# Transposing the softmax output P by DMA in three of four head groups, in a two-layer attention and FFN kernel on one Trainium2 core

## The chip, the cores and the metric

The kernel runs on one core of one Trainium2 chip. The metric is the time of one execution on the device, in microseconds (us). Before the change the median of three runs is 2704.88 us (2704.35 to 2705.86). A change of less than about 0.2%, 5.4 us, can't be told from none.

The core has five engines that run side by side and meet through semaphores: PE (TensorE) multiplies matrices and writes to PSUM, DVE (VectorE) and ACT (ScalarE) work on PSUM and SBUF, POOL (GpSimd) works on SBUF, and SP (SyncE) issues DMAs here. Each engine takes its instructions in order.

## What is computed

Two passes of the same two layers over 2048 rows of 576 numbers: attention with a recurrent memory, then a gated FFN. The attention works on 64 segments of 32 rows. Each segment sees 8 memory rows and itself, 40 rows in all, and the first 8 rows of its output are the memory of the next segment, so segments of one layer run one after another.

```python
for s in range(n_seg):                                  # 64 segments
    h = concat([mem, x[:, s*32:(s+1)*32]], axis=1)      # 8 + 32 rows
    q, k, v = (einsum('btd,dhe->bhte', h, W) for W in (Wq, Wk, Wv))   # 32 heads of 128
    scores = where(mask, einsum('bhqe,bhke->bhqk', q, k) * scale, -1e9)
    p = softmax(scores)
    o = einsum('bhqk,bhke->bhqe', p, v)
    o = einsum('bhte,hed->btd', o, Wo)
    mem = o[:, :8]
    outs.append(o[:, 8:])
...
x = x + A(layernorm(x)); x = x + B(layernorm(x))        # B: (silu(x w1) * (x w3)) w2, F = 4608
x = x + A(layernorm(x)); x = x + B(layernorm(x))
```

## The kernel before, in words

**Steps.** The kernel walks 72 steps `t`. Step `t` does segment `t` of the first attention and segment `t - 8` (`LAG`) of the second, so that their two recurrences run at the same time. In steps 8 to 63 both are there (56 steps "with two layers", `both(t)`); the first and last 8 steps have one. In a two-layer step the 40 rows of one layer's segment lie in partitions 0 to 39 and those of the other in 64 to 103, and the columns of a matmul are 80 instead of 40. `role(t)` alternates and says which places in the key rows the two layers use. The FFN of 128 rows at a time is woven between the steps.

**A group.** The 32 heads of a step are four groups `g` of eight (`NG`, `GH`). For each group, `step(t)` makes these nodes: QK and QKt (projections, two units a group), SC (scores into a PSUM bank), then on DVE the add of the mask (`sm_add`), the maximum and its subtraction (`sm_max`), on ACT the exponential (`sm_exp`), on DVE the sum, its reciprocal (`sm_sum`) and the scaled write of P as bf16 into the tile `PB` (`sm_pb`). `PB` has 128 key columns for each head; only those columns that belong to a row's own layer are written, the others must be zero, and so POOL clears the buffer after each use (`pb_zero`). There are two `PB` buffers.

**Transposing P.** The product of P and V needs P with keys in partitions. `ptr` (TR) does this on PE: eight matmuls a group with the P of one head as the stationary side and the tile `fold` (two identity matrices, one above the other) as the moving side, 40 columns each. The sum of both layers' rows comes out in one PSUM bank; since a key belongs to one layer only, `pt_ev` (PTe) copies the bank twice into the tile `PTS`, each time scaled by a 0 or 1 for each partition (`slots`) so that each layer keeps its own keys. ACT or DVE makes these copies, whichever the planner chooses. `pv` (PV) multiplies V and `PTS`, then come the copy into `OT` and the output projection WO, WOt.

**The order.** `make_nodes` lists all nodes with their needs, buffers and a planned duration. PE's order isn't planned: it is written out as a string of letters, `FIRST + FOUR * 11 + LAST`, one letter for a node (Q, q, S, T, P, O, o for attention, F, f, W, w for the FFN, X, x, V, v, G, g for V, and so on). `FOUR` holds four steps. `plan` takes that order and places the nodes of the other engines by their planned durations; the order within ACT, DVE, POOL and SP is the result, and the tile framework adds the semaphores. "AD" nodes may go to ACT or DVE.

**Queues around the change.** SP issues the weight loads of the FFN (`load_w13`: four DMAs, `load_w2`: one) into two buffers each, when PE has freed them, and the loads of rows of x. The planner has one queue "DMA" for it. POOL's queue issues the residual rows and the stores and holds the memsets of `PB`.

**PE's tile shapes.** A matmul with 128 rows and 128 columns of weights uses the whole array. Tails with 64 rows go in pairs side by side (64*128), and some others are split into two halves of 64 columns (128*64) where the neighbours already use that shape. Node modes such as `full/col` let `plan` pick the shape that the neighbours have.

Of the kernel before, what the change touches and what calls it, by code (L numbers as in the profile page):

```python
# [34 lines left out]
POOLS = {"bank": 8, "qkt": 4, "sme": 2, "pb": 2, "pts": 1, "ot": 4,  # L35
# [158 lines left out]
def ewh(*ns):  # L194
# [5 lines left out]
    "maQQQqqQqqSQqTqSqQQQqSSvVXxPTPTOPOTOoPooOoQqqqqQQSQqqvSVQQTQSqqPQOTSPoXTOPToxPOOooQqqqqQQSQQSvqVQTqqQSQqPSaOTPTO"  # L200
    "PTooPOOooQQqqqqQSQVvSqqQQQqqQTSSPXTOPTOPoToxPOOooQQpQqqVvqqSnQQSfFFqqfQQqSTQqfPFTWPSFTOOooPFTffPOOooWQqqqqQQFSQF"
    "SQffqVvqqQWTQSFxfqfQFSPXTWPFTfOPOTFPOOooooWQqfqQQSFQfqqVvSQqqfFWTQqfQSFPQqfTOSPFOTWPFTOPfoooOoFfqqQQQSWQqqvVSFfq"
    "qQQTWqqSQQPTSOoPbaOTXPxTOPooxOoXqqpQQQSVqqnQvfFSTQqqQQPSFfqqfQTFOPSWTFfPOOTFPWOooooffFQQQqqqWSGFfgqQQqfFSTQPQQqq"
    "qfFSWGTSfgGPFggTGOPOTFPOOooooWVvfqqQQQSFqqffFQQWTSFfqqQPQfqqSFQWTOfPSTaFoOPWOTFPffFOoooWQQqqqqQSbQgqqGSQQTQPQTgq"
    "qSGSOPGggTGPOTOPoooOoQqqppQQQSvqqVnnQQqqSFSffqTFQPQqWTFSPffOwTFPOTFPOWOwooooFffqqQQQSWwQFfgqqGSFqqfQQTWQPQSFffqq"
    "FGTgSwPGfggTGPFTOPOWOOowoooFqqfQQwWQaQfqqSFSvVfqqQFQTFqqfPQTQwSWFSfPOOTFPwTWffFPOOooooWwqqqQQQbSQqqgqGSQTQPQQqgq"
    "TSGSGPggGTOPOTOPoooOo"
# [5 lines left out]
LAST = (  # L213
    "QQpQqqqQSqQpnQqqVvTSSnQFffqqFPQTOwPoSWTffFPFTOPOOoooFqqqfQQwWQQfqfSFSFqGQQqqgTQQPWwFqgfTSSGGPFfggfFTGOPOTWPOOwoF"
    "oooFfqqfQQQwvSqqVQQWQqqSFTSqfqQPQWTOPSwFTFPffOTOwPWOooooFFqqffQQwQQqqvSWVSFqqfQQTWPQTqqSVQvPOSTbOPxwOoTooPOoXqQp"
    "QpqqvVQSQqqnQnSQQqqFTSfqfPQTOPSFTFPOWTOPwOooooFqffqQQQSQQqqqvVSTQQqqFSffqFPQWSwTFPffTOPFOTwPOOoWoooFqfqqQQQFSQfq"
    "xvXVwWSTFPQffqqQWQTSwFFPfqqQOSwWTFOPffTFPOWOwooooFQQvfqqVqqQSQWFSwFffqqQQQSTWQqPqTPSOTOPowOToboPxOoXqqqQQQpSvVqq"
    "qQQSnQTFfqQFSPfqQOSTFfPowTFPfOTOPFOfooowQQqqqfQQSqFSVvqqQwQFTSQffqqQPFTSXPwTOPOTFPOOooooFfxfVvqqQQQSQqqqfQSFQqqq"
    "QSTQwSPFTOffPFTOPwTOPfooOooFQqqqQQSqqqQQSQvVQTSfFQqqPwTFSPfTOFPOTOPoofOoopwFnfffFFwFwfffFFFwffFFwffFFwffFFwfFffF"
    "wFwfffFFFfww"  # L220
# [11 lines left out]
def make_nodes(em, nseg, pools, o=Opt, dma_bw=230e3, load_bw=400e3):  # L232
# [26 lines left out]
    ld_m0 = node("ACT", 0.1, em.load_m0(), prio=-90, name="m0", lat=2.5)  # L259
    ld_t = [load("ldt", kb(3 * R64, 4096), -10.0, em.load_tails(0)), node("ACT", 0.1, em.load_tails(1), prio=-120, name="ldt", lat=6.0)]  # L260
    node("ACT", 0.1, em.load_tails(2), prio=-80, name="ldt", lat=6.0)
# [48 lines left out]
    def v_nodes(name, t, k, prio, tail_at, emit, strips, deps, tail_deps, free):  # L310

        modes = ("col", "quad") if strips[0][3] == R64 else ("c32", "oct")
        b = banks()
        m_ = node("PE", 8 * 0.2158, emit(b, False), deps=deps, prio=prio, mode=modes[0], acq=b, name=name)
        n = node("PE", 0.2158, emit(b, True), deps=deps + tail_deps, prio=prio + tail_at, mode=modes[1], acq=b, name=name + "t")
        reads_ht.setdefault(t, []).extend([m_, n])
        for r in (0, 1):
            outs = em.v_parts(strips, r)
            b[r].users = len(outs)
            for p0, width, row, blk in outs:  # L320
                e = node("AD", (0.49, 0.6), em.v_ev(b[r], p0, width, row, blk), deps=[m_, n] + free.get(blk // 2, []), prio=prio + 0.01 * (blk // 2),
                         rel=[b[r]], name=name + "e")
                vx_ev.setdefault((name, t, blk // 2), []).append(e)
        return [m_, n]
# [16 lines left out]
    def vg_out(t, g, b, deps, row):  # L341

        return [node("AD", (0.49, 0.6), em.v_ev(b[r], row, R64, row, 2 * g + r), deps=deps, prio=t + o.vm + 0.01 * g + (0.05 if row == 0 else 0.0), rel=[b[r]],
                     name="VGe") for r in (0, 1)]

    def vx_pair(t, prio):
# [5 lines left out]
        for k in ((0, 1) if both(t) else (0,)):  # L352
            v_nodes("VX", t, k, prio + 0.01 * k, o.vxt, (lambda k: lambda b, tail: em.vx(t, k, b, tail))(k), em.vx_strips(t, k), deps, [], free)

    def step(t):
# [17 lines left out]
        for g in range(NG):  # L373
# [25 lines left out]
            pbs = node("DVE", w, em.sm_pb(t, g, sme, pb), deps=[d], prio=pf, acq=[pb], rel=[sme], name="pb", lat=0.125 if nl == 2 else 0.225)  # L399
# [26 lines left out]
            me[f"SC{g}"], me[f"TR{g}"], me[f"PV{g}"], me[f"WO{g}"] = sc, tr, pv, wo  # L426
# [100 lines left out]
    def x_in(g):  # L527
        xn = Slot("xn")
        ld = node("DMA" if g else "ACT", 0.8 if g else 0.1, em.load_xn(g, xn), deps=reads_ht.get(4 * g - 3, [])[:1], prio=4 * g - 3.0 if g else -100, acq=[xn],
                  name="ldxn", lat=2.5)  # L530
# [31 lines left out]
SW = 2 * QW  # L562

# [4 lines left out]
class Emitter:  # L568
# [431 lines left out]
    def sm_pb(self, t, g, sme, pb):  # L1000
        def f(n):
            for kd, key, c0, w in self.p_at(t):
                rs = slice(64 * kd, 64 * kd + QW)
                X, rec = self.T.SME[rs, sme.i], self.T.STAT[rs, sme.i]
                self.v("tensor_tensor", self.T.PB[rs, pb.i, :, c0:c0 + w], X[:, :, key:key + w],
                       rec.unsqueeze(2).to_broadcast([QW, GH, w]), op=ALU.mult)
        return f

    def pb_zero(self, pb):
        return lambda n: self.ch("POOL", self.nc.gpsimd.memset(self.T.PB[:, pb.i], 0.0))  # L1010
# [4 lines left out]
    def ptr(self, t, g, pb, b):  # L1015

        def f(n):
            for j in range(GH):
                self.mm(self.bk(b)[:, j * QW:(j + 1) * QW], self.T.PB[0:104, pb.i, j, :], self.T.fold[0:104, :], True, True)
        return f  # L1020

    def pt_ev(self, t, g, m, b, pts):

        def f(n):
            src = self.bk(b)[:, 0:GH * QW]
            if not self.both(t):
                w = 4 * QW
                self.cp(n, self.T.PTS[:, pts.i, 0, m * w:(m + 1) * w], src[:, m * w:(m + 1) * w])
                return
            dst = self.T.PTS[:, pts.i, m, :]  # L1030
            keep = self.T.slots[:, role(t), m ^ role(t):(m ^ role(t)) + 1]
            if n.by == "ACT":
                self.act(dst, src, ACT.Copy, scale=keep)
            else:
                self.v("tensor_scalar", dst, src, keep, None, op0=ALU.mult)
        return f

    def pv(self, t, g, pts, b):
        def f(n):
            nq = self.nq(t)  # L1040
            for j in range(GH):
                self.mm(self.bk(b[j // 4])[:, (j % 4) * nq:(j % 4 + 1) * nq], self.T.V[:, self.head(g, j) // 4, (self.head(g, j) % 4) * E:(self.head(g, j) % 4 + 1) * E],
                        self.T.PTS[:, pts.i, 0:nq // QW, j * QW:(j + 1) * QW], True, True)
        return f

# [66 lines left out]
    def yts(self, t, ls, tail):  # L1112
        def f(n):
            yT, _ = self.yT(t)
            for li in ls:
                j = (t - LAG * li) % 4
                c0 = self.ycol(t, self.kind(t, li), False)
                if not tail:
                    self.cp(n, self.T.YTS[:, li, 0:4, j * SEG:(j + 1) * SEG], yT[:, 0:4, c0:c0 + SEG])
                else:  # L1120
                    self.v("tensor_tensor", self.T.YTS[R64:P, li, 4, j * SEG:(j + 1) * SEG], yT[0:R64, 4, c0:c0 + SEG],
# [3 lines left out]
    def post_tr(self, li, g, b):  # L1125
        def f(n):

            for db in (4, 3, 2, 1, 0):
                d0 = min(db * P, D - P)
                self.mm(self.bk_bf(b, D)[:, d0:d0 + P], self.T.YTS[:, li, db, :], self.T.ident[:, 0:P], True, True, is_transpose=True)  # L1130
# [79 lines left out]
def kernel(  # L1210
# [41 lines left out]
    T.fold = sp.tile([P, QW], BF, name="fold")  # L1252

    T.slots = sp.tile([P, 2, 2], F32, name="slots")

# [29 lines left out]
    nc.gpsimd.memset(T.fold[:], 0.0)  # L1285
    for r in (0, R64):
        nc.gpsimd.affine_select(out=T.fold[:], in_=T.fold[:], compare_op=ALU.not_equal, fill=1.0, base=-r,
                                pattern=[[-1, QW]], channel_multiplier=1)

    nc.gpsimd.memset(T.slots[:], 0.0)  # L1290
    for e, kd, lo, hi in ((0, 1, 24, 80), (1, 0, 72, 112)):
        inside, outside = T.slots[:, e, kd:kd + 1], T.slots[:, e, 1 - kd:2 - kd]
        nc.gpsimd.memset(inside, 1.0)
        nc.gpsimd.affine_select(out=inside, in_=inside, compare_op=ALU.is_ge, fill=0.0, base=-lo, pattern=[[0, 1]], channel_multiplier=1)
        nc.gpsimd.affine_select(out=inside, in_=inside, compare_op=ALU.is_ge, fill=0.0, base=hi - 1, pattern=[[0, 1]], channel_multiplier=-1)
        nc.gpsimd.tensor_scalar(outside, inside, -1.0, 1.0, op0=ALU.mult, op1=ALU.add)

# [54 lines left out]
```

## Time and profile before

| what | value | how to read it |
|---|---|---|
| median of three runs | 2704.88 us | unprofiled comparisons |
| profiled execution | 2708.0 us, span 2705.0 us | the span is from first to last instruction |
| granted PE clock | 0.997 of full | no throttling |
| PE, DVE, ACT, POOL busy | 2618.6, 2097.7, 1401.6, 334.1 us | PE is the busiest by far |
| transposes on PE, 104*128 and 104*64 | 1816 and 976 records | fold,PB in the rows; split ones count twice |
| copies PTS on ACT | 315 at 531 ns, 97 at 303 ns | two-layer and one-layer steps |
| copies PTS on DVE | 133 at 550 ns, 31 at 320 ns | the same |
| memset of PB on POOL | 288 at 951 ns | one for each group |
| DMA queue of SP | 305.43 MB, 38.5% of 16 engines | nearly all weight loads |
| a repeated period of four steps | 157.03 us | 1170.72 to 1327.75 us in the trace |

Busy times on PE are unions of pipelined matmuls, so the length of one record (180 ns and more) is a latency. What a matmul costs in a stream is the distance between the starts of two neighbours.

### The profile page before, as it was taken

The numbers are of one execution on the slowest core, as the hardware profiler recorded it, in microseconds if no ns is written. First come the engines' busy times: TensorE is split into PE (matmuls) and PEld (weight loads), VectorE is DVE, ScalarE is ACT, GpSimd is POOL, SyncE is SP. The second block draws the span as 40 slices with busy tenths as digits, with TensorE's granted clock in tenths as the row PEclk, the third lists the DMA queues.
The fourth block names the chain that finished last, engine by engine and source line by source line (L and its number), as shares of the span: only waits on it lengthen the run. The fifth ranks groups of instructions, "written<-read, shape, count | busy, mean of one in ns | idle before, by whom it ended". The sixth has DMA issues, their size and how long they took to land.

```text
span 2705.0 us, 135792 instructions
## 1 busy us (share of the span) xinstructions
PE 2618.6 (97%) x60482; PEld 2272.3 (84%) x60523; DVE 2097.7 (78%) x5423; ACT 1401.6 (52%) x3978; POOL 334.1 (12%) x411
## 2 busy tenths in 40 slices
PE   5999999999999999999999999999999999999998
PEld 4788888888888888888888888888888888888886
DVE  5777887787788778777877877787777777777876
ACT  2655554554555555554555555455545546554452
POOL 1111110110111011011101101010111101011110
PEclk9999999999999999999999999999999999999999
DMA  9064524244342434434243433423343342334457
GB/s 316 7 182 118 158 82 128 80 119 116 104 124 85 116 90 119 117 108 128 76 119 88 127 108 108 134 80 110 94 124 106 108 139 70 112 93 130 129 166 245
DMA packets 478171, 321.99 MB, mean 119 GB/s; under 512 B 26024, under 2 KB 467760, under 8 KB 476944
## 3 DMA queue, kind: packets, MB, share of 16 engines
q1 hardware_dynamic: 474048, 305.43, 38.5%
q8 instruction: 473, 7.75, 1.2%
q0 software_dynamic: 3024, 6.93, 0.9%
q10 hardware_dynamic: 512, 0.94, 0.2%
q14 instruction: 114, 0.93, 0.1%
HBM read 308.49 MB, written 2.36 MB: 115 GB/s over the span
## 4 chain that ended last, share of the span: by engine, by line
PE 80%; DVE 9%; ACT 6%; issue 2%; DMA 2%; SPq 1%; POOL 0%; ACTq 0%; DVEq 0%; POOLq 0%
PE bank L591 80%; ACT V L594 3%; DVE STAT L597 2%; DVE PTS L597 2%; ACT PTS L594 1%; DVE V L597 1%; DVE SME L597 1%; DVE PB L597 1%; DMA W<-in_A_Wk_dram 1%; DVE HTT L597 1%; SPq L600 1%; DMA W<-in_B_w_dram 1%; ACT HT L594 0%; ACT QKT L594 0%; DMA WV<-in_A_Wv_dram 0%
## 5 line engine op out<-in xcount | busy, mean ns | idle before, releaser
L591 PEld LDWEIGHTS <-W 128*128 128x128 bf16 (+2 forms) x31904 | 1258.2, 100 | 128.8 <-issue 68.7
L591 PE MATMUL bank<-HT,W 128*128 128x80 bf16 (+3 forms) x23040 | 799.9, 196 | 16.8 <-issue 7.3
L591 PE MATMUL bank<-XTB,W 128*64 128x256 bf16 (+5 forms) x8864 | 662.6, 263 | 5.9 <-DMA W<-in_B_w_dram 3.0
L594 ACT ACTIVATE QKT<-bank 128x256 bf16<-128x256 f32 (+2 forms) x1524 | 349.5, 311 | 363.5 <-PE bank L591 320.7
L1010 POOL MEMSET PB<- 128x1024 bf16 x288 | 273.9, 951 | 1944.5 <-PE bank L591 1242.7
L591 PE MATMUL bank<-OT,WO 128*128 128x80 bf16 (+2 forms) x11520 | 401.6, 198 | 2.2 <-issue 1.8
L594 ACT ACTIVATE V<-bank 32x512 bf16<-32x512 f32 (+1 forms) x609 | 347.8, 586 | 90.4 <-PE bank L591 81.6
L591 PEld LDWEIGHTS <-WO 128*128 128x128 bf16 (+1 forms) x11520 | 376.8, 102 | 13.7 <-issue 4.4
L591 PE MATMUL bank<-WV,HT 128*32 128x512 bf16 (+5 forms) x3728 | 362.3, 381 | 3.8 <-issue 2.2
L591 PE MATMUL bank<-W2C,HTT 128*128 128x288 bf16 (+1 forms) x2776 | 318.4, 286 | 2.9 <-issue 1.8
L597 DVE TENSOR_REDUCE STAT<-SME 104x8 f32<-104x320 f32 (+1 forms) x576 | 274.0, 476 | 25.2 <-ACT SME L594 18.9
L597 DVE TENSOR_TENSOR PB<-SME,STAT 40x128 bf16<-40x128 f32 (+4 forms) x912 | 275.5, 336 | 9.7
L594 ACT ACTIVATE HTT<-bank 128x512 bf16<-128x512 f32 (+1 forms) x324 | 175.3, 550 | 185.9 <-PE bank L591 183.9
L591 PEld LDWEIGHTS <-HT 128*32 128x32 bf16 (+4 forms) x3768 | 164.1, 99 | 119.5 <-issue 20.3
L597 DVE SCALAR_TENSOR_TENSOR XR<-bank,XR 128x288 f32<-128x288 f32 x576 | 243.7, 448 | 23.3 <-PE bank L591 17.4
L591 PEld LDWEIGHTS <-HTT 128*128 128x128 bf16 (+1 forms) x2840 | 222.4, 103 | 42.2 <-issue 4.5
L597 DVE SCALAR_TENSOR_TENSOR HTT<-HTT,bank 128x512 bf16<-128x512 bf16 (+1 forms) x324 | 201.0, 620 | 59.0 <-ACT HTT L594 56.2
L594 ACT ACTIVATE OT<-bank 128x320 bf16<-128x320 f32 (+1 forms) x392 | 147.0, 403 | 173.0 <-PE bank L591 146.3
L597 DVE CAST QKT<-bank 128x192 bf16<-128x192 f32 (+4 forms) x524 | 140.5, 315 | 117.7 <-PE bank L591 117.3
L597 DVE TENSOR_TENSOR HTT<-HTT,bank 128x512 bf16<-128x512 bf16 (+1 forms) x324 | 203.6, 628 | 28.5 <-PE bank L591 0.9
L594 ACT ACTIVATE PTS<-bank,slots 128x320 bf16<-128x320 f32 x315 | 157.0, 531 | 128.8 <-PE bank L591 95.0
L594 ACT ACTIVATE SME<-SME 104x320 f32<-104x320 f32 (+1 forms) x288 | 135.5, 470 | 100.2 <-DVE SME L597 95.5
(69 smaller groups left out, 1856.8 us busy)
## 6 DMA issues: line engine op xcount, KB each, us to landing
W<-in_B_w_dram SPq DMA_DIRECT2D x612, 256.0 KB, 3.6
W2C<-in_B_w_dram SPq DMA_DIRECT2D x306, 288.0 KB, 3.3
W<-in_B_w_dram SPq DMA_DIRECT2D x612, 32.0 KB, 3.5
W<-in_B_w_dram SPq DMA_DIRECT2D x8, 1024.0 KB, 12.2
W<-in_A_Wq_dram SPq DMA_DIRECT2D x9, 512.0 KB, 9.5
WO<-in_A_Wo_dram SPq DMA_DIRECT2D x4, 1152.0 KB, 16.7
XR<-in_A_x_dram POOLq DMA_DIRECT2D x16, 288.0 KB, 2.8
WV<-in_B_w_dram SPq DMA_DIRECT2D x4, 1152.0 KB, 10.9
```

Of the source, the lines that this page charges most:

```text
L591: self.ch("PE", self.nc.tensor.matmul(out, lhsT=lhsT, rhs=rhs, start=start, stop=stop, skip_group_check=True, **k))
L594: self.ch("ACT", self.nc.scalar.activation(*a, **k))
L597: self.ch("DVE", getattr(self.nc.vector, fn_)(*a, **k))
L600: self.ch("SP", self.nc.sync.dma_start(out=out, in_=in_))
L1010: return lambda n: self.ch("POOL", self.nc.gpsimd.memset(self.T.PB[:, pb.i], 0.0))
```

## The change

P of groups 0, 1 and 2 of a two-layer step goes from `PB` to `PTS` by one transposing DMA on SP's queue, in line with the weight loads: 112 partitions x 1024 columns of `PB` become 128 partitions x 8 heads x 112 columns. Since the DMA keeps the two layers' rows apart (columns 0 to 39 and 64 to 103), PV reads its 80 columns out of the 112 (`pcols`), and no copy through PSUM is made. Group 3, and all groups of the one-layer steps, are transposed on PE, now with a piece of the identity matrix (`ident`) that picks 80 columns, so that the layers come out apart and plain copies do; `fold` and `slots` are gone. The transposes of group 3 take two banks.

`PB` is one buffer instead of two, `PTS` two instead of one, and POOL clears `PB` once in each step but the first (71 times), because all groups of a step write the same columns. `YO` now lies in spare columns of `YTS`. The letters of the order are all new, and some planned durations differ.

```diff
+DMA_GROUPS = 3
+TRD, TRL = 0.6, 4.2
-POOLS = {"bank": 8, "qkt": 4, "sme": 2, "pb": 2, "pts": 1, "ot": 4,
+POOLS = {"bank": 8, "qkt": 4, "sme": 2, "pb": 1, "pts": 2, "ot": 4,
...
-    "QqqpQQpQqqVvnSSnQFfqfqFQQQTfqqSFPWTFPSwTfFOOPWTwPOOooooFqqffQQQQfqqSFGSgqfFTQQPwQTQqqqgGSWPFGSfggfFOTGPOwTOPWOoo"
-    "ooFqfqqQQwWQQVqvSaSFFffqqQQwQQqqSTWSFPffTFOPWwTOFPffTOFPwWOooooFfqqqQQWQQSqqqQSQQbQqgqSTGGPSgTGPOTggGPOTwPOOoooo"
+    "QppQqqVSqqvQQnnQSFqfqqQQSFqffQFQwPWPSFffFOOPwTWPOOooooFfqqfQQFQQqqSWwFSGfqgqQQQPQqqfWSwFSGFfgggGPGPOOTFPOOooooWwF"
+    "qffqQQQQqqSFWSVqfqvQQwFQqqffFSPQwFPWSffOOFPwTOPWOooooFqqfQQqqaSQQWSQQqqqqQQbSwGSgggGPGPOgGPOTOPoooOo"
...
-                e = node("AD", (0.49, 0.6), em.v_ev(b[r], p0, width, row, blk), ...
+                e = node("AD", (0.56, 0.6), em.v_ev(b[r], p0, width, row, blk), ...
...
+            if g == 0 and t:
+                zero = [node("POOL", 0.95, em.pb_zero(pb), deps=last_pt, prio=pf, acq=[pb], name="pbz")]
+            else:
+                zero = []
...
-            bt = Slot("bank", users=2)
-            tr = node("PE", 8 * 0.0258, em.ptr(t, g, pb, bt), deps=[pbs], prio=pf + o.tr, mode="full/col", acq=[pts, bt], name="TR")
-            node("POOL", 0.95, em.pb_zero(pb), deps=[tr], prio=pf, rel=[pb], name="pbz")
-            pe_ = [node("AD", (0.425, 0.46) if nl == 2 else ew(160), em.pt_ev(t, g, m, bt, pts), deps=[tr], prio=pf, rel=[bt], name="PTe") for m in (0, 1)]
+            if nl == 2 and g < DMA_GROUPS:
+                pe_ = [node("DMA", TRD, em.ptd(t, g, pb, pts), deps=[pbs], prio=pf, acq=[pts], rel=[pb], name="TRD", lat=TRL)]
+                last_pt[:] = pe_
+            else:
+                bt = banks(nl)
+                tr = node("PE", 8 * (0.0258 if nl == 1 else 0.0358), em.ptr(t, g, pb, bt), deps=[pbs], prio=pf + o.tr, mode="full/col", acq=[pts] + bt, rel=[pb], name="TR")
+                pe_ = [node("AD", ew(320), em.pt_ev(t, g, i, b, pts), deps=[tr], prio=pf, rel=[b], name="PTe") for i, b in enumerate(bt)]
+                last_pt[:] = [tr]
...
+PQ = 112
...
+    def ptd(self, t, g, pb, pts):
+        return lambda n: self.ch("SP", self.nc.sync.dma_start(out=self.T.PTS[:, pts.i], in_=self.pbt(pb)[0:PQ].rearrange("p h k -> p (h k)"),
+                                                                 transpose=True))
...
+    def pcols(self, t, g, pts, j):
+        P_ = self.T.PTS[:, pts.i, j, :]
+        if not self.both(t) or g >= DMA_GROUPS:
+            return P_[:, 0:self.nq(t)]
+        v, e = P_[:, 0:1], role(t)
+        return bass.AP(v.tensor, v.offset + R64 * e, [list(x) for x in v.ap][:-1] + [[R64 - P * e, 2], [1, QW]])
...
-    T.PB = sp.tile([P, pools["pb"], GH, P], BF, name="PB")
-    T.PTS = sp.tile([P, pools["pts"], 2, GH * QW], BF, name="PTS")
+    T.PB = sp.tile([P, GH, P], BF, name="PB")
+    T.PTS = sp.tile([P, pools["pts"], GH, PQ], BF, name="PTS")
...
-    T.YO = sp.tile([R64, 2 * QW], F32, name="YO")
-    T.YTS = sp.tile([P, 2, 5, P], BF, name="YTS")
+    T.YTS = sp.tile([P, 10, P], BF, name="YTS")
+
+    T.YO = T.YTS[0:R64, 8:10, :].rearrange("p a b -> p (a b)").bitcast(F32)[:, 0:2 * QW]
```

More of the change, by code (lines that the diff above doesn't have):

```diff
@@ L199 @@
 FIRST = (
[L200 to L204, printed above, removed]
@@ L215 @@
[L215 to L219, printed above, removed]
@@ L257, in load @@
         return node("DMA", nbytes / load_bw, fn, deps=deps, prio=prio, name=name, lat=2.0)
-    ld_m0 = node("ACT", 0.1, em.load_m0(), prio=-90, name="m0", lat=2.5)
-    ld_t = [load("ldt", kb(3 * R64, 4096), -10.0, em.load_tails(0)), node("ACT", 0.1, em.load_tails(1), prio=-120, name="ldt", lat=6.0)]
-    node("ACT", 0.1, em.load_tails(2), prio=-80, name="ldt", lat=6.0)
+    node("DMA", 4.0, lambda n: None, prio=-999.0, name="boot")
+    ld_m0 = node("ACT", 0.6, em.load_m0(), prio=-90, name="m0", lat=8.0)
+    ld_t = [load("ldt", 1.7 * kb(3 * R64, 4096), -10.0, em.load_tails(0)), node("ACT", 0.6, em.load_tails(1), prio=-120, name="ldt", lat=8.0)]
+    node("ACT", 0.6, em.load_tails(2), prio=-80, name="ldt", lat=10.0)
     ld_h = [load("ldqk", kb(512, 4096), half - 9.0, em.load_qk(half)) for half in (0, 1)]
@@ L320, in v_nodes @@
             for p0, width, row, blk in outs:
-                e = node("AD", (0.49, 0.6), em.v_ev(b[r], p0, width, row, blk), deps=[m_, n] + free.get(blk // 2, []), prio=prio + 0.01 * (blk // 2),
+                e = node("AD", (0.56, 0.6), em.v_ev(b[r], p0, width, row, blk), deps=[m_, n] + free.get(blk // 2, []), prio=prio + 0.01 * (blk // 2),
                          rel=[b[r]], name=name + "e")
@@ L341, in vg_out @@
     def vg_out(t, g, b, deps, row):
-        return [node("AD", (0.49, 0.6), em.v_ev(b[r], row, R64, row, 2 * g + r), deps=deps, prio=t + o.vm + 0.01 * g + (0.05 if row == 0 else 0.0), rel=[b[r]],
+        return [node("AD", (0.56, 0.6), em.v_ev(b[r], row, R64, row, 2 * g + r), deps=deps, prio=t + o.vm + 0.01 * g + (0.05 if row == 0 else 0.0), rel=[b[r]],
                      name="VGe") for r in (0, 1)]
@@ L528, in x_in @@
         xn = Slot("xn")
-        ld = node("DMA" if g else "ACT", 0.8 if g else 0.1, em.load_xn(g, xn), deps=reads_ht.get(4 * g - 3, [])[:1], prio=4 * g - 3.0 if g else -100, acq=[xn],
-                  name="ldxn", lat=2.5)
+        ld = node("DMA" if g else "ACT", 0.8 if g else 0.6, em.load_xn(g, xn), deps=reads_ht.get(4 * g - 3, [])[:1], prio=4 * g - 3.0 if g else -100, acq=[xn],
+                  name="ldxn", lat=2.5 if g else 9.0)
         ht_set(0, g, ln_nodes("L0", xn, xn, [ld], 4 * g - 2.0 if g else -8, ht_writes(0, g)))
@@ L1017, in f, with pt_ev @@
         def f(n):
+            nq, v, e = self.nq(t), self.T.ident[0:104, 0:1], role(t)
+            I = bass.AP(v.tensor, v.offset + R64 * e, [list(x) for x in v.ap][:-1] + [[R64 - P * e, 2], [1, QW]]) if nq == SW else self.T.ident[0:104, 0:QW]
             for j in range(GH):
-                self.mm(self.bk(b)[:, j * QW:(j + 1) * QW], self.T.PB[0:104, pb.i, j, :], self.T.fold[0:104, :], True, True)
+                k = j * nq % (4 * SW)
+                self.mm(self.bk(b[j * nq // (4 * SW)])[:, k:k + nq], self.pbt(pb)[0:104, j, :], I, True, True)
         return f
-    def pt_ev(self, t, g, m, b, pts):
+    def pt_ev(self, t, g, i, b, pts):
         def f(n):
[L1025 to L1035, printed above, removed]
+            nq = self.nq(t)
+            h = GH * QW // nq
+            self.cp(n, self.T.PTS[:, pts.i, h * i:h * (i + 1), 0:nq], self.bk(b)[:, 0:4 * SW].rearrange("p (h q) -> p h q", h=h))
         return f
@@ L1118, in f @@
                 if not tail:
-                    self.cp(n, self.T.YTS[:, li, 0:4, j * SEG:(j + 1) * SEG], yT[:, 0:4, c0:c0 + SEG])
+                    self.cp(n, self.T.YTS[:, 4 * li:4 * li + 4, j * SEG:(j + 1) * SEG], yT[:, 0:4, c0:c0 + SEG])
                 else:
-                    self.v("tensor_tensor", self.T.YTS[R64:P, li, 4, j * SEG:(j + 1) * SEG], yT[0:R64, 4, c0:c0 + SEG],
+                    self.v("tensor_tensor", self.T.YTS[R64:P, 8 + li, j * SEG:(j + 1) * SEG], yT[0:R64, 4, c0:c0 + SEG],
                            self.T.YO[:, c0:c0 + SEG], op=ALU.add)
@@ L1129, in f @@
                 d0 = min(db * P, D - P)
-                self.mm(self.bk_bf(b, D)[:, d0:d0 + P], self.T.YTS[:, li, db, :], self.T.ident[:, 0:P], True, True, is_transpose=True)
+                self.mm(self.bk_bf(b, D)[:, d0:d0 + P], self.T.YTS[:, 4 * li + db if db < 4 else 8 + li, :], self.T.ident[:, 0:P], True, True, is_transpose=True)
         return f
@@ L1250 @@
     T.ident = sp.tile([P, P], BF, name="ident")
-    T.fold = sp.tile([P, QW], BF, name="fold")
-    T.slots = sp.tile([P, 2, 2], F32, name="slots")
     T.maskb = sp.tile([P, 2, QW], BF, name="maskb")
@@ L1284 @@
                             pattern=[[-1, P]], channel_multiplier=1)
[L1285 to L1296, printed above, removed]
     nc.gpsimd.memset(T.maskb[:], 0.0)
```

33 lines of the change are left out of this document (23 added, 10 removed).

## The prediction

> **What bounds the kernel now.** I read the page from the top: busy shares first, then the chain that ended last.
>
> ```profile
> PE 2618.6 (97%) x60482; PEld 2272.3 (84%) x60523; DVE 2097.7 (78%) x5423; ACT 1401.6 (52%) x3978; POOL 334.1 (12%) x411
> ...
> PE 80%; DVE 9%; ACT 6%; issue 2%; DMA 2%; SPq 1%; POOL 0%; ACTq 0%; DVEq 0%; POOLq 0%
> ```
>
> PE is busy 97% of the span and makes 80% of the last chain. So a matmul taken off PE shortens the kernel by its pitch, as long as nothing makes PE wait instead. What the transposes cost PE is in its timeline (start, length, instructions), in step 30:
>
> ```profile
> 1114.18 0.45 PE L591 MATMUL bank<-PTS,V 128*128 128x80 bf16 x8
> 1114.47 2.13 PE L591 MATMUL bank<-W2C,HTT 128*128 128x288 bf16 x16
> 1116.43 0.36 PE L591 MATMUL bank<-fold,PB 104*128 104x40 bf16 x8
> 1116.64 1.31 PE L591 MATMUL bank<-OT,WO 128*128 128x80 bf16 x32
> ...
> 1119.53 0.45 PE L591 MATMUL bank<-PTS,V 128*128 128x80 bf16 x8
> 1119.91 0.61 PE L591 MATMUL bank<-XTB,W 64*128 64x256 bf16 x8
> ```
>
> Lengths overlap, because matmuls are pipelined; the starts count. The eight 40-column transposes (fold,PB) take 1116.43 to 1116.64, 0.21 us. Eight 80-column matmuls take 0.29 us (1114.18 to 1114.47). The same eight followed by a matmul of another tile shape (64*128) take 0.38 us (1119.53 to 1119.91): a change of tile shape costs about 0.10 us.
>
> Then the waits, of the queue that gets the new work and of PE:
>
> ```profile
> SPq L600 <- PE bank L591: 1852.3, 696, 74.8
> ```
>
> ```profile
> PE bank L591 <- ACT PTS L594: 12.3, 20, 1.9
> ...
> PE bank L591 <- DVE PTS L597: 5.4, 20, 1.0
> ```
>
> The columns are total us, times, longest. SP stands 1852 us waiting for PE to free weight buffers, so it has time to issue more. PE waits 17.7 us in all for copies of P into PTS. Four steps of the repeated order last 157.03 us on the chip (adds of the scores at 1170.72 and 1327.75). At the pitches above, with 55 changes of shape, its matmuls make 152.0 us, so about 5 us in each such period are waits and jitter.
>
> **The change, part by part.** Transposes removed: before, 288 groups at 0.21 us, 60.5 us. After, 56 groups (the fourth of each of the 56 steps with two layers) with 80 columns at 0.285 us, 16.0 us, and 64 groups of the one-layer steps at 0.21 us, 13.4 us. Together 29.4 us: -31.1 us.
>
> Order searched anew: in the built instruction order of PE, tile shapes change 1179 times before and 1260 after. 81 more at 0.10 us: +8.1 us. The counts of all other matmuls are the same but for halves and wholes of one shape, which cost alike, and twelve 512-column dummies fewer in the first step; these stand under the first weight loads (DMA share 1.01 in the first 60 us), so 0. If that cover were gone they would be worth 12 x 0.43 us, 5 us.
>
> Copies of P out of PSUM: 576 become 176. ACT had 315 at 531 ns and 97 at 303 ns; DVE 133 at 550 and 31 at 320. None bounds the kernel; what they free shows only in PE's 17.7 us of waits for PTS. The plan hands DVE 58 more V copies (685 ns, 40 us) instead. I take 0; bounds are -17.7 us (all of these waits gone) and 0. POOL's 217 memsets fewer (951 ns) lie on an engine at 12%: 0. YO moved into spare columns of YTS: its writer can now wait for POST's transposes, which come about once in two steps, with at least half a step until the next YO; 0, and up to about 0.5 us per POST, 16 us, if it were exposed.
>
> The DMA itself. One transfer moves 112 x 1024 x 2 bytes, 224 KB. The trace has no transposing DMA and none within SBUF. The nearest rows, from issue to landing:
>
> ```profile
> W<-in_B_w_dram SPq DMA_DIRECT2D x612, 256.0 KB, 3.6
> W2C<-in_B_w_dram SPq DMA_DIRECT2D x306, 288.0 KB, 3.3
> ...
> WO<-in_A_Wo_dram SPq DMA_DIRECT2D x4, 1152.0 KB, 16.7
> ...
> out_dram<-XN POOLq DMA_DIRECT2D x15, 144.0 KB, 2.7
> ```
>
> I call D the time from the last write of PB until the transposed P can be used: hand-over to SP, issue, landing. Its bounds are 2.7 us (the small store) and 16.7 us (a load in the crowded start). Nearest in size and queue are 3.3 and 3.6 us; with 0.1 us for each hand-over and up to 0.9 us behind two issues already running (two W2C issues take 0.89 us in SP's timeline) I take 4.5 us. A row of 112 short pieces may be slower than a row of weights; nothing here says by how much.
>
> [...]
>
> What D may be: PB is now one buffer, so group g+1's PB is written only after group g's DMA has landed. The softmax chain from scores to PB is, in rows, 0.48 + 0.48 + 0.49 + 0.47 + 0.48 + 0.20 + 1.12 = 3.7 us, 4.3 with hand-overs. I laid PE's new order out at the pitches above. In the repeated four steps, with S end and PV start in us:
>
> - Step 1: S 0.2, 5.3, 10.5, 18.7; PV 16.8, 18.1, 25.1; TR 26.3. In time while D is below 6.0.
> - Step 2: S 40.5, 44.4, 53.8, 56.7; PV 50.5, 62.9, 65.0; TR 67.5. First group: 40.5 + 4.3 + D up to 50.5, D below 5.7.
> - Step 3: S 82.7, 85.6, 97.5, 103.3; PV 97.4, 101.7, 107.9; TR 109.2. D below 6.1.
> - Step 4: S 119.4, 123.0, 129.0, 131.9; PV 134.5, 136.5, 140.1; TR 141.5. Three DMAs in a row with a 1.2 us write of PB between: 119.4 + 4.3 + 3D + 2.4 up to 140.1, D below 4.7.
>
> So D = 4.5 hides under PE's other matmuls: 0. Beyond 4.7, step 4 loses 3 us for each us, steps 1 to 3 together 5 more beyond about 6. Over 14 such periods: D of 5.0 costs 14 us, 5.5 costs 35, 6.0 costs 60, 7.0 costs 190. Where DVE waits to write PB, the next copies of QKT, V and HTT stand behind it, and PE's QK and FF for them.
>
> SP: 168 more issues at 0.45 to 0.6 us, 76 to 100 us, against 1852 us of waiting. Weight loads stand behind a transpose that waits for PB; pairs of buffers give each about 2.5 us of room (FF chunks 157/18 = 8.7 us apart, four issues 2.6 us, landing 3.6 us). I take 0.
>
> Sum: -31.1 + 8.1 = -23.0 us on the profiled span of 2705.0: 2682. The median of the runs is 2704.88, 0.1 us away, so nothing is corrected. Below 0.2% (5.4 us) a difference can't be told from none.
>
> **Rivals.** *Relief:* ACT, DVE and PSUM lose 400 copies, and PE's waits for PTS vanish too: 2682 - 17.7 = 2664. For: step 4 of the shown period loses 0.8 us before one PV. Against: DVE keeps its load. *Eaten up:* D is 5.0 to 5.5; 14 to 35 us come back: about 2705. For: room in step 4 is 0.2 us. *Late transposes:* the one PB buffer is the mechanism, with D of 6: each group's DMA delays the next group's PB, PE waits before PV, +60: 2742. It decides from D = 5.3, where the waits pass 23 us. For: an unmeasured kind of DMA on a queue with bursts of eight loads. Against: the 288 KB rows. *Block by block:* if the transfer goes out as eight blocks, one for each head, each with an issue of 0.45 us before the last one's 3.3 us to land, D is 6.9. Step 4 then loses 3 x (6.9 - 4.7) = 6.6 us, the others 2.5, 1.2 and 2.2, a period 12.5: +175, 2857. For: no row shows such a DMA. Against: each weight load is many short rows too, and issues in 0.45 us. [...] *Weights late:* the change only moves the wait, SP's head is held by transposes beyond the 2.5 us of room, by 0.5 us for half of the 18 chunks: +63, 2745.
>
> **How the numbers follow.** Forecast 0.48, relief 0.11, eaten up 0.12, late transposes 0.19, block by block 0.04, weights late 0.06. Faster: 0.48 + 0.11 + half of eaten up, 0.06 = 0.65. Same: 0.05 of eaten up. Slower: the rest, 0.30. The time is 2682. The forecast's own range is 2672 to 2692 (switch cost 0.08 to 0.12 us, dummies, some jitter). The whole range goes from 2662, below relief, to 2746, which takes in late transposes with D up to 6 and leaves out the longer ones and block by block.
>
> **What would show it.** PE rows with PB: 56 groups of 80 columns and 64 of 40, some 29 us from start to start. Landing of the PTS issues: 3.5 to 4.5 us if right, over 5.3 if the late rival holds. Waits of PE for DMA PTS: below 20 us in all. The period of four steps: 155.4 us (150.4 laid out, plus 5). PE's waits for W unchanged (3.0 us). Wrong would be a period at or above 157.0 us, or waits of DVE PB for DMA PTS that pull HTT and QKT copies behind them.

## The result, and the profile after

The changed kernel takes 2687.45 us (median of four runs, 2683.80 to 2691.46), the kernel before beside it 2705.37 us (2704.35 to 2709.18): ratio 0.9935, 95% interval 0.9922 to 0.9947. Measured a second time, later, it took 2682.02 us, ratio 0.9921 (0.9906 to 0.9937). So it is 18 to 22 us faster; 2682 was forecast. The profiled execution after lasted 2686.17 us, its span 2684.2 us.

Page of the changed kernel: the parts of busy time, of the queues, of the chain, and of the DMA issues (KB each, median us to landing).

```profile
PE 2593.0 (97%) x58657; PEld 2234.0 (83%) x58700; DVE 2086.2 (78%) x5352; ACT 1260.1 (47%) x3649; POOL 130.1 (5%) x182
...
q1 hardware_dynamic: 629952, 343.99, 48.0%
...
PE 82%; DVE 6%; DMA 6%; ACT 3%; issue 2%; SPq 1%; ACTq 0%; POOL 0%; DVEq 0%; POOLq 0%
...
W<-in_B_w_dram SPq DMA_DIRECT2D x612, 256.0 KB, 3.7
```

PE is busy 25.6 us less (2618.6 before), and its share of the chain rises from 80 to 82%. But the share of DMA in that chain rises from 2 to 6%: more of that chain now runs through a DMA. SP's queue moves 343.99 MB, 38.6 more than before (305.43), as much as 168 transfers of 224 KB; the loads themselves land as before (3.7 us, 3.6 before).

The view of the tile PTS in the changed kernel (duration min/median/max in ns, then first and last start) shows the new instruction, and how long its data takes.

```profile
L1028 SPq DMA_TRANSPOSE PTS<-PB x168: 1222/1240/2626, 244.2 to 2391.5; - x168
...
DMA to landing us min/median/max: 2.6/2.8/5.5
```

Issuing a transposing DMA holds SP for 1.24 us in the median, where a load of W takes 0.51 and one of W2C 0.42. From issue to landing it takes 2.8 us. With the hand-over, D (last write of PB to P in place) has a median of 2.99 us over the 147 transposes whose landing is recorded, three quarters are below 4.20, nine in ten below 4.64, and the longest is 5.92.

What PE waited for, in the changed kernel (total us, times, longest); the last line is of the kernel before:

```profile
PE bank L603 <- DMA W<-in_B_w_dram: 18.9, 21, 1.9
...
PE bank L603 <- DMA W2C<-in_B_w_dram: 2.3, 7, 0.5
...
PE bank L603 <- ACT PTS L606: 1.1, 2, 0.6
...
PE bank L603 <- DMA PTS<-PB: 0.5, 2, 0.4
```

```profile
PE bank L591 <- DMA W<-in_B_w_dram: 3.0, 3, 2.3
```

Three readings. PE hardly waits for the transposed P (0.5 us). Its waits for copies into PTS fell from 17.7 us to 1.1. And its waits for weights rose from 3.0 us to 18.9, and 2.3 more for W2C. What holds the weights up is in SP's waits:

```profile
SPq L612 <- PE bank L603: 907.8, 607, 77.5
SPq L1028 <- DVE PB L609: 673.9, 138, 21.5
```

L612 is the line of the loads, L1028 that of the transposes. SP stood 1852.3 us waiting to load; now it stands 907.8 us, and 673.9 us at the head of its queue with a transpose whose P isn't written, up to 21.5 us at a time. The loads behind can't start, though their buffers may be free. The timeline of the changed kernel shows one case (start, length, engine; in brackets the idle time before, and what ended it):

```profile
1166.16 1.12 DVE L609 TENSOR_TENSOR PB<-SME,STAT 40x128 bf16<-40x128 f32 x4
...
1166.34 1.91 PE L603 MATMUL bank<-XTB,W 128*64 128x256 bf16 x31
...
1167.35 1.44 SPq L1028 DMA_TRANSPOSE PTS<-PB  x1
...
1168.89 2.28 SPq L612 DMA_DIRECT2D W<-in_B_w_dram  x4
...
1174.86 2.44 PE L603 MATMUL bank<-XTB,W 64*128 64x256 bf16 x20 [0.87 <-DMA W<-in_B_w_dram]
```

DVE ends PB at 1167.28, and SP issues its transpose from 1167.35 to 1168.79. Meanwhile PE makes the main matmuls on the weight buffer that the next four loads will fill: 31 of 32 are in the row at 1166.34, the first starts at 1166.30. In no_trd (experiment 2) the first of such loads starts 1.6 us after such matmuls begin. Here the loads stand behind the transpose and start at 1168.89, 2.6 us after them. The third load, with the last 64 rows of its matrix, is issued at 1170.02 and lands at 1174.81 by the trace; the matmuls that need it start at 1174.86, 0.87 us late.

Where the time went by stage, from the starts of the first adds of the scores of steps 0, 8 and 64 in each trace (us; the transposes by DMA are in steps 8 to 63 alone):

| stretch | before | after | after, again | without transposes |
|---|---|---|---|---|
| start to step 8 | 244.3 | 240.1 | 239.8 | 238.8 |
| steps 8 to 63 | 2182.3 | 2169.7 | 2165.4 | 2138.0 |
| step 64 to end | 278.4 | 274.4 | 274.8 | 278.8 |

The last column is the experiment no_trd, below. In the steps that the change is about, 12.6 to 16.9 us are gained, and some 8 us outside of them.

### The profile page after: what moved, and what is told of

Its sections match the earlier page's. It is cut to its first block, busy times and chain, and to the rows that moved or that the text cites. A ratio compares the mean times of both kernels' runs of the same rounds, so it can differ in the third digit from the quotient of the medians.

```text
span 2684.2 us, 132015 instructions
## 1 busy us (share of the span) xinstructions
PE 2593.0 (97%) x58657; PEld 2234.0 (83%) x58700; DVE 2086.2 (78%) x5352; ACT 1260.1 (47%) x3649; POOL 130.1 (5%) x182
## 3 DMA queue, kind: packets, MB, share of 16 engines
q1 hardware_dynamic: 629952, 343.99, 48.0%
## 4 chain that ended last, share of the span: by engine, by line
PE 82%; DVE 6%; DMA 6%; ACT 3%; issue 2%; SPq 1%; ACTq 0%; POOL 0%; DVEq 0%; POOLq 0%
PE bank L603 82%; DMA W<-in_B_w_dram 3%; DVE V L609 1%; DVE STAT L609 1%; DMA W2C<-in_B_w_dram 1%; ACT V L606 1%; DVE SME L609 1%; SPq L612 1%; DVE HTT L609 1%; DVE XR L609 1%; DVE PB L609 1%; DMA WV<-in_A_Wv_dram 0%; DMA PTS<-PB 0%; ACT YTS L606 0%; ACT SME L606 0%
## 5 line engine op out<-in xcount | busy, mean ns | idle before, releaser
L603 PE MATMUL bank<-XTB,W 128*64 128x256 bf16 (+5 forms) x9120 | 668.5, 263 | 22.1 <-DMA W<-in_B_w_dram 18.9
L606 ACT ACTIVATE QKT<-bank 128x256 bf16<-128x256 f32 (+4 forms) x1546 | 356.7, 312 | 296.0 <-PE bank L603 237.3
L603 PEld LDWEIGHTS <-WO 128*128 128x128 bf16 (+1 forms) x11520 | 375.6, 102 | 20.6 <-issue 11.5
L603 PE MATMUL bank<-WV,HT 128*32 128x512 bf16 (+4 forms) x3535 | 360.5, 384 | 9.2 <-issue 6.0
L606 ACT ACTIVATE V<-bank 32x512 bf16<-32x512 f32 (+1 forms) x551 | 317.9, 587 | 101.2 <-PE bank L603 91.6
L603 PE MATMUL bank<-W2C,HTT 128*64 128x288 bf16 (+1 forms) x3176 | 320.8, 286 | 3.7 <-DMA W2C<-in_B_w_dram 2.3
L609 DVE TENSOR_REDUCE STAT<-SME 104x8 f32<-104x320 f32 (+1 forms) x576 | 275.3, 478 | 14.3 <-ACT SME L606 7.3
L603 PEld LDWEIGHTS <-HT 128*32 128x32 bf16 (+4 forms) x3576 | 153.7, 99 | 136.0 <-issue 27.3
L603 PEld LDWEIGHTS <-HTT 128*64 128x64 bf16 (+1 forms) x3240 | 229.1, 105 | 39.6 <-issue 6.5
L609 DVE SCALAR_TENSOR_TENSOR XR<-bank,XR 128x288 f32<-128x288 f32 x576 | 244.3, 449 | 12.8 <-PE bank L603 8.8
L609 DVE CAST V<-bank 64x512 bf16<-64x512 f32 (+1 forms) x313 | 213.6, 683 | 22.3 <-PE bank L603 15.1
L609 DVE CAST QKT<-bank 128x128 bf16<-128x128 f32 (+2 forms) x502 | 137.0, 315 | 83.0 <-PE bank L603 81.5
L609 DVE TENSOR_TENSOR SME<-bank,maskb 104x320 f32<-104x320 f32 (+1 forms) x288 | 139.0, 483 | 32.7 <-PE bank L603 27.4
```

The source lines that it names most:

```text
L603: self.ch("PE", self.nc.tensor.matmul(out, lhsT=lhsT, rhs=rhs, start=start, stop=stop, skip_group_check=True, **k))
L606: self.ch("ACT", self.nc.scalar.activation(*a, **k))
L609: self.ch("DVE", getattr(self.nc.vector, fn_)(*a, **k))
```

## The experiments

The question: of what PE gained by the removed transposes, how much comes back, and through what: through P that comes late, through the issue time of the DMA, through its traffic, or through the loads behind it? Each time stands beside runs of the kernel before on the same chip.

**1. before_no_tr: the removal alone.** The kernel before, with its order, doesn't transpose groups 0 to 2 of the two-layer steps.

```diff
-            for j in range(GH):
+            for j in range(0 if self.both(t) and g < 3 else GH):
                 self.mm(self.bk(b)[:, j * QW:(j + 1) * QW], self.T.PB[0:104, pb.i, j, :], self.T.fold[0:104, :], True, True)
```

> The kernel before, without the eight matmuls that transpose P in groups 0 to 2 of the 56 two-layer steps (168 groups); the copies to PTS stay and read whatever stands in the bank, so the output is another. The order and its 1179 changes of tile shape stay. My theory: these matmuls cost PE their pitch, 168 x 0.21 us = 35 us, so 2705 becomes about 2670. Rival: part of them stood in time that PE would have waited anyway (waits for PTS and V copies follow them), then it is under 20 us, above 2685.

Measured: 2685.85 us against 2704.85, ratio 0.9925 (0.9911 to 0.9940), 19 us. 168 groups at 0.21 us are 35 us. Its waits of PE say where part of the other 16 went:

```profile
PE bank L591 <- ACT PTS L594: 14.0, 19, 1.9
...
PE bank L591 <- ACT V L594: 8.5, 27, 2.1
...
PE bank L591 <- DVE PB L597: 6.5, 18, 0.7
PE bank L591 <- DVE PTS L597: 6.5, 21, 1.0
```

Before, these four were 12.3, 5.4, 2.6 and 5.4: 10 us more. A PE that runs ahead meets the softmax and the copies earlier. The rival held, at the edge of its range: in this order the pitch of the removed matmuls was an upper bound of their worth. The remaining 6 us are not explained.

**2. no_trd: the changed kernel without the DMA.** Its 168 transposes aren't issued; all else stays in its order. (PTS is cleared once at the start, 0.8 us on DVE, here and in plain_copy.)

```diff
     def ptd(self, t, g, pb, pts):
-        return lambda n: self.ch("SP", self.nc.sync.dma_start(out=self.T.PTS[:, pts.i], ...
+        return lambda n: None
```

> The changed kernel without its 168 transposing DMAs; P of those groups is not transposed and the output is another. PE's order is the same. My theory: PE's 21 us of waits for weights come from SP, which holds the loads behind transposes (1.24 us of issue each, 674 us of waiting for PB); without them these waits fall to about 5 us and the span to some 2668. Rival: the weight waits come from the new order of FF and W2 on PE alone; then the span stays within 4 us of 2684.

Measured: 2656.74 us, ratio 0.9817 (0.9801 to 0.9834), lower than the theory said. SP's waits for PE are 1821.5 us, and PE's for W:

```profile
PE bank L603 <- DMA W<-in_B_w_dram: 2.5, 2, 2.3
```

So the transposes, meant to be hidden, cost 31 us in the changed kernel (2687.45 - 2656.74; by the stages 31.7 us in steps 8 to 63). Against its second measurement it is 25 us (27.4 by the stages). Of the 31.7 us, 20.6 are PE's waits for weights in these steps (18.3 for W, 2.3 for W2C, against none listed without the transposes). An estimated 3.4 are a lower clock, shown at the end of this text. The rest, some 8 us, stands in no row of its own.

**3. trd_no_pb: the same DMA without its wait.** SP's order, the number of transposes, their size and target stay; the source is a piece of WO that never changes, in place of PB, so they don't wait for the softmax (they still wait for a free PTS).

```diff
-        ... in_=self.pbt(pb)[0:PQ].rearrange("p h k -> p (h k)"),
+        ... in_=self.T.WO[0:PQ].rearrange("p h d -> p (h d)")[:, 0:GH * P],
```

> The changed kernel with its 168 transposing DMAs reading the weights WO in place of PB; same size, same places in SP's order, but SP need not wait for the softmax. The output is another, since P of those groups isn't used. If weights are late because SP's head waits for PB (674 us) with loads behind it: PE's 21 us of waits for weights fall under 6 and the time to some 2660, near the kernel without transposes (2657). If SP's issue time (168 x 1.24 us) or the traffic is the cause: the weight waits stay at 15 us or more and the time within 6 us of 2687.

Measured: 2656.47 us, ratio 0.9821 (0.9807 to 0.9836), as without any transpose. The views of its tile PTS and of its waits:

```profile
L1028 SPq DMA_TRANSPOSE PTS<-WO x168: 1222/1254/2830, 227.1 to 2356.8; - x168
...
DMA to landing us min/median/max: 2.9/4.0/5.6
```

```profile
PE bank L603 <- DMA W<-in_B_w_dram: 4.1, 4, 2.4
```

The same 1.25 us of issue, 168 times, and the same traffic cost nothing that can be measured. All of the 31 us hang on the wait for PB at the head of SP's queue. (DVE's writes of PB don't wait for the transfers here either, but that was only 2.0 us in the changed kernel.)

**4. plain_copy: the wait with a shorter issue.** A plain DMA of 112 x 896 elements from PB to PTS in place of the transpose; it waits for PB as the transpose does.

```diff
-        return lambda n: self.ch("SP", self.nc.sync.dma_start(out=self.T.PTS[:, pts.i], ... transpose=True))
+        return lambda n: self.dma(self.T.PTS[0:PQ, pts.i], self.pbt(pb)[0:PQ, :, 0:PQ])
```

> The changed kernel with a plain DMA copy (112 x 896 elements of PB) in place of each transposing one, so P is not transposed. It still waits for PB in SP's order. If the transposing itself is dear (issue 1.24 us, 128 rows of short pieces): the copies issue in about 0.55 us, land in about 2.5 us, and the time falls by 5 to 15 us. If the wait for PB at SP's head is what counts: within 5 us of 2687.

Measured: 2667.68 us, ratio 0.9863 (0.9848 to 0.9877). Its copies in the view of PTS, and two of its waits:

```profile
L612 SPq DMA_DIRECT2D PTS<-PB x168: 589/637/1955, 242.7 to 2370.8; - x168
...
DMA to landing us min/median/max: 2.6/2.8/4.8
```

```profile
SPq L612 <- DVE PB L609: 722.2, 143, 22.2
```

```profile
PE bank L603 <- DMA W<-in_B_w_dram: 7.3, 6, 2.2
```

SP stands as long for PB (722 us) and the landing is the same 2.8 us, but the kernel is 20 us faster than the changed one: more than expected. Lighter traffic doesn't show as the reason: the 256 KB loads land in 3.8 us here, 3.7 in the changed kernel. So the wait and the issue act together: a load that is ready while SP stands at a transpose loses the rest of that wait and then the issue. Of the 31 us, 20 go with the transposing issue behind such a wait (1.24 us for 0.64), 11 stay with the shorter one; by the second measurement of the changed kernel 14 of 25 go.

**5. w2_on_pool: the W2 loads leave SP's queue.** 306 of the loads go to POOL's queue, to stand behind no transpose.

```diff
-    lds.append(node("DMA", kb(256, 576) / dma_bw, em.load_w2(pr_, w2), prio=prio - 0.99, ...
+    lds.append(node("SWD", kb(256, 576) / dma_bw, em.load_w2(pr_, w2), prio=prio - 0.99, ...
...
-        return lambda n: self.dma(self.T.W2C[:, w2.i], ...
+        return lambda n: self.swdma(self.T.W2C[:, w2.i], ...
```

> The changed kernel with the 306 loads of W2 moved from SP's queue to POOL's, which the change left at 5% busy. If SP's order (a load behind a transpose that waits for PB) makes weights late: waits for weights fall by half, 6 to 14 us off the changed kernel. If the DMA engines' load is the cause (48% against 38% of 16 engines): no change within 4 us, since the same bytes move. If POOL's own issues delay its other work (the LN power, the memset of PB), new waits of DVE for POOL appear and it is slower.

Measured: 2708.80 us, ratio 1.0017 (1.0001 to 1.0033): 21 us slower than the changed kernel, a miss. PE waits 27.8 us for W and 6.6 for W2C. None of the three forecasts held: the waits rose, and DVE waits 0.2 us for POOL. SP stands longer at the transposes (788.6 us), with its remaining loads still behind them. Part of the loss is the clock: it is granted at 0.50 for 27.3 us of steps 8 to 63, against 6.8 in the changed kernel. The planner also orders the other queues anew here, so this run doesn't isolate the W2 loads, and why W comes later still stays open.

**6. trd_on_act: the transposes leave SP's queue.** ACT issues them; the planner was given the measured issue time, 1.24 us, and the same 4.8 us in all as before.

```diff
-TRD, TRL = 0.6, 4.2
+TRD, TRL = 1.24, 3.56
...
-                pe_ = [node("DMA", TRD, em.ptd(t, g, pb, pts), ...
+                pe_ = [node("ACT", TRD, em.ptd(t, g, pb, pts), ...
...
-        return lambda n: self.ch("SP", self.nc.sync.dma_start(out=self.T.PTS[:, pts.i], ...
+        return lambda n: self.ch("ACT", self.nc.scalar.dma_start(out=self.T.PTS[:, pts.i], ...
```

> The changed kernel with the transposing DMAs issued by ACT, 1.24 us each of its time in the plan and 3.56 us more to land; PE's order stays. If SP's order alone makes weights late: waits for weights under 5 us, and the time 5 to 20 us below 2687. Rival: ACT then waits for PB in its own order, with the copies of QKT, V and OT behind it, and PE waits for ACT instead: 10 us or more above 2687.

Measured: 2701.57 us, ratio 0.9994 (0.9982 to 1.0006). The weights are on time, and P is late instead:

```profile
PE bank L603 <- DMA PTS<-PB: 17.1, 16, 3.2
...
PE bank L603 <- ACT OT L606: 6.8, 15, 1.0
```

D is 4.35 us in the median here, 5.9 at nine in ten. ACT's own order is not what makes it long: nine in ten transposes are issued within 0.1 us after P is written. They land later, by the view of PTS:

```profile
DMA to landing us min/median/max: 2.6/4.3/8.2
```

SP now issues weight loads beside them. The 38 transposes with no such load in the 3.5 us before them or during their issue land in 2.65 us (median), the 71 with four or more in 4.9 us. The time is in the rival's range, but PE's waits for ACT, its mechanism, are the smaller part. The run also changes the planner's numbers, and the next pair shows that these same numbers alone cost as much (2702.04 us); so what the queue itself is worth stays open.

**7 and 8. plan_measured and plan_issue: only the planner's numbers.** The changed kernel planned `TRD, TRL = 0.6, 4.2` (issue, and latency after it). These two plan 1.24, 1.5 and 1.24, 3.56.

> The changed kernel with the planner told what the trace shows of a transposing DMA: 1.24 us of SP's time and 1.5 us more to land, in place of 0.6 and 4.2. PE's order stays, the orders of SP, DVE, ACT and POOL follow. If weights are late because the planner puts SP's issues where SP has no time for them: waits for weights under 12 us, the time down 5 to 12 us against the changed kernel. Rival: the order of PE is fitted to 4.8 us and the other engines' orders hardly matter: within 4 us.

> The changed kernel with the planner told SP's true time for a transpose, 1.24 us, while the time until P is there stays at 4.8 us (1.24 + 3.56). The run with 1.24 + 1.5 lost 18 us. If it lost them because the plan then expects P and PB 2 us too early: this one is at or below 2687 (0 to -10). If any other order of SP and DVE than the searched one loses: 2695 or more.

Measured: 2705.55 us (ratio 1.0003, 0.9991 to 1.0016) and 2702.04 us (0.9993, 0.9982 to 1.0004). Planning with truer times loses all of the gain; of the forecasts, only the last one (2695 or more) held. The first allows 2.74 us from the start of the issue to the landing, near the measured median, where the changed kernel's plan allows 4.8: PE waits 14.4 us for P. The second keeps 4.8 and only plans SP as busy as it is: PE still waits 13.1 us for P, and 16.0 for W. PE's letters are the same in all three, and what differs is the planner's order on the other queues. That these letters suit one such order alone is a reading; no run has letters made for the true times.

**9 and 10. later_0 and later_12: SP's order alone.** All other queues keep their order. 70 and 99 of the transposes are moved behind one to three of the loads that follow them on SP, where the trace said that those loads were ready first.

```diff
+LATER = {6: 1, 20: 1, 26: 2, ...}
...
+        for _ in range(LATER.get(k, 0)):
+            j = next(j for j in range(i + 1, len(order)) if order[j].eng == "DMA")
...
+            order.insert(j, order.pop(i))
...
-    for n in plan(nodes, pools, ORDER):
+    for n in later(plan(nodes, pools, ORDER)):
```

> The changed kernel with SP's order alone altered: 70 of the 168 transposes go behind one to three of the weight loads that followed them, there where the traces (of the changed kernel, and of the one without transposes for when a load could start) let those loads be issued before PB is written. The result is the reference's. My theory, loads held at SP's head by transposes that wait for PB: waits for weights fall from 21 us to under 8, the time from 2687 to about 2665. Rival (a moved transpose lands later behind the load's data and PE waits for P instead): PE's waits for PTS come up by 10 us or more and the time stays within 6 us of 2687 or above.

> The same with 99 transposes moved, those included that this delays by up to 1.2 us. If only the loads' lateness counts: at or some us below the run with 70 (2655 to 2665). If the room of the transposes is used up (D may be 4.7 us in the tightest step, it is 3.0 in the middle now): above the run with 70, with PE waiting for PTS.

Measured: 2709.86 us (ratio 1.0021, 1.0011 to 1.0031) and 2734.29 us (1.0102, 1.0080 to 1.0124). In later_12, by its waits of PE and of DVE:

```profile
PE bank L618 <- DMA PTS<-PB: 36.5, 26, 3.4
...
PE bank L618 <- DMA W<-in_B_w_dram: 7.8, 10, 2.4
```

```profile
DVE PB L624 <- DMA PTS<-PB: 86.2, 60, 3.7
```

The waits for weights do fall (18.9, then 14.0 and 7.8 us), but P is late: D's median is 4.37 and 4.82 us, nine in ten below 6.52 and 7.33, and DVE stands 55.3 and 86.2 us in front of the one PB buffer. The rival of later_0 held, and so did the second case of later_12. This is also the mechanism of the prediction's rival "late transposes". These runs cost 22 and 47 us over the changed kernel's 2687.45. The prediction's price list is for one D in all steps (+35 us at 5.5, +60 at 6), and here D spreads, while the loads gain at the same time; so the list itself isn't tested.

**11 and 12. later_slack, and the changed kernel again.** Only the 21 moves whose P in the trace of the changed kernel stood ready at least 2.0 us before anything needed it; and the changed kernel beside it.

> The changed kernel with 21 of the 168 transposes moved behind the one or two weight loads that follow them on SP, only those whose P in the trace of after stood ready at least 2.0 us before the next write of PB and the next PV (nearly all 70 of the first such list had less than the 2.3 us that one chunk of loads takes to issue). Theory (the loss is the loads' waiting behind transposes, and slack can pay for it): 21 of 70 places free at most 31 x 21/70 = 9 us, so 2678 to 2686 us; PE waits for W 12 to 17 us (18.9 in after), for DMA PTS below 4. Rival (DVE's and SP's order has no slack anywhere, since each later P moves the next PB and with it all copies behind it): 2690 to 2700, PE waits for DMA PTS 5 to 12 us.

> The changed kernel itself once more, unaltered, beside the former on the same chip: all theories say what was measured first, 2684 to 2691 us, 0.9922 to 0.9947 of the kernel before; it shows how far apart two measurements of one program lie, and so what the variants' differences of 2 to 9 us are worth.

Measured: 2688.73 us (ratio 0.9947, 0.9933 to 0.9961), and 2682.02 us (0.9921, 0.9906 to 0.9937) for the changed kernel. Here is what moved in later_slack:

```profile
PE bank L618 <- DMA W<-in_B_w_dram: 11.8, 15, 2.3
...
PE bank L618 <- DMA PTS<-PB: 5.3, 6, 1.9
```

```profile
DVE PB L624 <- DMA PTS<-PB: 12.4, 13, 2.2
```

In the second profile of the changed kernel these are 15.2 us, none and 1.3 us. Where the loads gain 5.9 us (3.4 for W, 2.5 for W2C), P loses 5.3 us: no gain, and the medians of the two lie 6.7 us apart while their intervals overlap. The time is just below the rival's range, its waits for P are the rival's. The changed kernel came out 2 us below the range that was expected of it. The program measured twice gave medians 5.4 us apart, so differences of that size between variants carry no weight here.

No version tried beats the changed kernel while it still computes P for all groups.

## Why the prediction was right, point by point

The direction, the size and the hiding of the DMA were right. But terms that were put at nothing were not nothing, had opposite signs, and nearly cancelled: 25 to 32 us lost through SP's queue, against 21.5 us gained in the same steps and 8 us outside of them that no term held. That the total came out so near 2682 is luck.

- **Removed transposes, -31.1 us:** their rows are as said. A group of eight with 80 columns takes 0.29 us from start to start in the timeline of the changed kernel:

```profile
1189.09 0.45 PE L603 MATMUL bank<-ident,PB 104*128 104x80 bf16 x8
1189.38 1.15 PE L603 MATMUL bank<-W2C,HTT 128*128 128x288 bf16 x8
```

  But "a matmul taken off PE shortens the kernel by its pitch, as long as nothing makes PE wait instead" had its condition broken in the old order (experiment 1: 19 of 35 us).
- **Shape changes, +8.1 us:** no run isolates them. Without the transposing DMAs, four steps last 153.9 to 154.3 us (steps 16 to 56), against the 150.4 us that were laid out.
- **Copies of P, "I take 0; bounds are -17.7 us (all of these waits gone) and 0":** this size failed. The waits went to 1.1 us, so 16.6 of the 17.7 us vanished, as the rival "relief" said; whether by fewer copies or by the new order, no run separates. (Its sign, 0.8 us before one PV of step 4, is 0.63 us in the trace.) In steps 8 to 63 the forecast was 14 periods x (157.03 - 155.4), 22.8 us. Without the transposing DMAs these steps are 44.3 us shorter: PE is busy 28.8 us less there (2152.3 to 2123.5), and idle 15.4 us less, of which 14.3 were waits for PTS.
- **D, taken as 4.5 us:** too high; 2.99 in the median. It hides, as forecast, and PE waits 0.5 us for P. "Eaten up" and "late transposes" fell for this order. "Block by block" fell: eight heads land in 2.8 us together.
- **SP, "168 more issues at 0.45 to 0.6 us, 76 to 100 us ... I take 0":** the step that failed. An issue takes 1.24 us (208 us in all), and the room of 2.5 us a load isn't enough while the head of the queue waits for PB. Price: 25 to 31 us (experiments 2 and 3). This is the rival "weights late"; it named the mechanism and put it at +63. Total waiting of 1852 us said nothing on this: this in-order queue has no time to spare while its head waits for something else, 673.9 us of it for PB.
- **The rest, 0:** start and end gave 8.2 us. The start gains 4.2 to 5.5 us in all three profiles of the new order in the table, about the 5 us that the twelve dummies were worth if uncovered; no run separates that. The 4 us at the end are absent without the transposes, and stay open.
- **The sum:** forecast -22.8 in steps 8 to 63; found -44.3 without the transposing DMAs and +31.7 with them: -12.6 us, and -8.2 outside, -20.8 on the span (2705.0 to 2684.2). How much of the -44.3 belongs to the two terms of the forecast, no run separates.
- **The signs it named:** P's waits (0.5 us) and the rows of PB were as said. The landing, 2.8 us, was below the 3.5 to 4.5 given. PE's waits for W, "unchanged (3.0 us)", were 18.9. The period, forecast at 155.4 us, is 154.8 to 157.1 in the twelve from step 12 to step 60, 156.1 in the mean: one of them (157.1) is past the 157.0 that would show it wrong.

## What to carry to other kernels

Price a DMA put into a shared in-order queue by two things: how long it stands at the head waiting for its input (673.9 us in all here), and how long its issue then takes (1.24 us each); the loads behind it lose both (PE's waits for W: 18.9 us, 3.0 before). Ask of the latest load behind it how much room it has, not of the queue how long it idles. And what a faster engine gains was seen here only with a new order: the removal alone gave 19 of 35 us, and the searched order gave all of its gain back with other planning numbers, or with 70 transposes moved behind the next loads.

## What the hardware showed that was not expected

**A transposing DMA is dear to issue, not to move.** 1.24 us of issue on SP for 112 x 1024 elements, against 0.64 us for a plain copy of 112 x 896; both land in 2.8 us.

**Two waits for weights were followed by a half clock.** Windows of the changed kernel (length, then busy us of PE; PEclk is the third number from the right):

```profile
258.00:264.50 6.50, 4.60 (x101) 4.07 (x100) 4.77 (x14) 1.51 (x4) 0.00 (x0) 1.00 0.95 184
264.50:267.90 3.40, 3.40 (x44) 3.40 (x44) 0.99 (x3) 0.82 (x2) 0.94 (x2) 0.50 0.92 280
267.90:274.00 6.10, 6.10 (x176) 5.67 (x174) 2.74 (x10) 1.62 (x6) 0.52 (x2) 1.00 0.88 243
```

In the first, PE stands 1.90 us for W before 264.03; then its clock is granted at 0.50 for 3.41 us, which costs an estimated 1.7 us more (half of 3.41). A second such window, 3.41 us at 0.50, follows at 326.0; there PE had waited 1.64 us for W before 325.04. A wait of 1.91 us for W before 1644.67 was followed by none, so what sets the half clock is not shown. The two windows are an estimated 3.4 of the 31.7 us that the transposes cost; in the rest of steps 8 to 63 the clock stays at 1.00. Without transposes, and with plain copies, these steps have no such window; in the slower versions 5 to 10 they take 6.8 to 27.3 us.
